# Softmax and the sum over P V by VectorE's 32x32 transposes in an attention decode kernel

## The chip, the cores and the metric

The kernel runs on one core of a Trainium2 chip. The metric is device time in microseconds for one execution of the whole program. The core's engines are called PE (TensorE matmuls; PEld is its weight load), DVE (VectorE), ACT (ScalarE), POOL (GpSimd) and SP (SyncE, which here only issues loads).

## What is computed

The reference is one decode step (one token, batch 8, width 512) of an attention layer followed by a small MLP.

```
x = A_x                                           # [8, 1, 512]
q = (layernorm(x) @ wq) as 32 heads of 128
k, v = the last 2048 positions of the caches, 8 kv heads, each shared by 4 q heads
p = softmax(q k^T / sqrt(128));  o = p v
h = x + o @ wo
y = layernorm(h)
x1 = y + (token shifts, all zero for one token)
h2 = gelu(layernorm(x1) @ w3) @ w4
out = h + x1 + h2
```

For each batch entry there are 32 rows of 2048 scores. The caches are bf16 and are read once: 2048 positions of 8 heads of 128 for K and V, 8 MB a batch, 64 MB in all, beside 4 MB each for wq and wo and 3.5 MB for w3 and w4.

## The kernel before

**Queues.** Every engine has a list of operations (`Engine.op`) that is written out in the order in which Python calls it; each engine runs its own list strictly in that order, and semaphore waits join the lists. All loads go out on SP's queue (`load_k`, `load_v`, `load_wo`, `load_wq`, `load_w3`, `load_w4`, L675 to L710) in the order of one string of letters, K and V alternating, then wo, w3 and w4. A K load is 2 MB: four kv heads. It goes into one of three slots and waits for the transposes (L323) of the load that had the slot. A V load has three slots too and waits for the P V product (L452) of three loads before. The last V goes into a K slot.

**Items.** A batch has two K loads and eight items, each a quarter of a load: `pe_T` turns 2048 rows of K with sixteen 128x128 transposes on PE (L323), `evict` copies them to SBUF, one half on ACT (L331) and one on DVE (L333), and `pe_QK` multiplies them with q (L343). The scores of a batch stand in one PSUM bank `S_ps[b % 2]` as 128 partitions x 512: 32 heads on 32 partitions, in four blocks of 32 partitions, and within a block in four groups `s`, so one head's scores lie in four of the partitions of a block.

**Softmax before.** `softmax_1` takes the maximum of each partition on DVE (L362). A head needs the maximum over its four partitions: `softmax_2` turns the column into a row with an fp32 matmul on PE (L366), joins the four on DVE (L368) and negates (L372); `softmax_3` turns the row back with another fp32 matmul (L376), copies it (L379), and ACT takes the exponential and its row sums (L380) into `P_sb`. `softmax_4` turns P with four PE transposes (L388) and a DVE copy (L392). `widen` multiplies by a matrix that repeats each row (L408, four matmuls of 512 columns) and masks the result with `own_f`, in three cases on DVE (L421) and in one on ACT (four operations at L418), giving `pT_sb`, the weights for P V. `softmax_5` sums L over the four partitions with an fp32 matmul (L425) and takes 1/L (L427).

**P V and O before.** `pe_PV` runs sixteen matmuls per half batch (L452) into `o_rows` or a free scores bank. The result holds four blocks of 128 columns, and each partition needs only one of them. ACT copies the bank as bf16 (L458), DVE subtracts for the low part (L459), and `pe_O` selects and adds blocks with eight matmuls (L469). DVE scales by 1/L and masks (L481) and adds four columns into `oW` (L487).

**Order.** The loop at L543 goes over items p and calls the parts of batch b at fixed distances from its last item: `A_WORK` and `B_WORK` (L538 to L541). The work of batch 6 is put back by four items (`LAG`, L542). `warm` (L429) and `warm_end` (L437) are matmuls whose result nothing uses; they stand in the last two batches and after them. `sm_pe` and `sm_dv` put the users of PSUM bank `sm` in one chain.

**After the attention.** With the last `oW` come wo (L498 to L531), the two layernorms, w3 (`pe_w3`, L608), Gelu on ACT (L634), w4 (L661), copies (L671, L673) and the store (L713). The residual rows enter the w4 sum through L651. POOL clears `qrow` for the MLP (L628) after the last O matmul.

Of the kernel before, what the change touches and what calls it, by code (L numbers as in the profile page):

```python
# [6 lines left out]
dt = mybir.dt  # L7
ACT = mybir.ActivationFunctionType
ALU = mybir.AluOpType
AX = mybir.AxisListType  # L10

B = 8
# [24 lines left out]
NPB = 3  # L37
ON_ACT = (1,)
# [36 lines left out]
def bass_sequential_preLN__sliding_block_cached__mixer_s_mlp__decode_kernel(  # L75
# [23 lines left out]
    with es:  # L99
# [8 lines left out]
        turn_b = sb([128, 128], dt.bfloat16, "turn_b")  # L108
        rows_f = sb([128, 64], dt.float32, "rows_f")
        heads_f = sb([128, H], dt.float32, "heads_f")  # L110
# [9 lines left out]
        sel_l = sb([128, 128], dt.float32, "sel_l")  # L120
        sel_o = sb([128, NS, 64], dt.bfloat16, "sel_o")
# [19 lines left out]
        P_sb = sb([128, NPB, 512], dt.bfloat16, "P_sb")  # L141
        pT_sb = sb([128, 2, NN, 128], dt.bfloat16, "pT_sb")
        PT_sb = sb([128, 512], dt.bfloat16, "PT_sb")
        wide = sb([128, KQ, 128], dt.bfloat16, "wide")
        mcol = sb([128, 1], dt.float32, "mcol")
        negcol = sb([128, B], dt.float32, "negcol")
        lcol = sb([128, B], dt.float32, "lcol")
        Mrow = sb([1, H], dt.float32, "Mrow")
        negrow = sb([1, 128], dt.float32, "negrow")
        rL = sb([128, B], dt.float32, "rL")  # L150
# [31 lines left out]
        O_ps = sm[:, 256:384]  # L182
        MROW = slice(384, 512)
        NEG = slice(384, 385)
        LB = slice(385, 386)
# [9 lines left out]
        def dma(eng, dst, src, sem, *waits):  # L195
            def f(e):
# [12 lines left out]
        e_ones = PO.op(lambda e: e.memset(ones_f[:], 1.0))  # L209
        e_qz = PO.op(lambda e: e.memset(qblk[:], 0.0))  # L210
# [20 lines left out]
        e_heads = DV.op(lambda e: e.tensor_reduce(heads_f[:, :].rearrange("p (t x) -> p t x", t=KQ),  # L231
                                                  ident_f[:, :].rearrange("p (t s x) -> p t x s", t=KQ, s=NS),
                                                  AX.X, ALU.add))
        a = ident_f[:, :]
        e_wd = DV.op(lambda e, a=a: e.tensor_copy(
            wide[:, :, :].rearrange("p n (a x) -> p (n a) x", x=KQ),
            bass.AP(tensor=a.tensor, offset=a.offset, ap=[a.ap[0], a.ap[1], [0, KQ]])))

        def spread(e, dst, src):
            a = src  # L240
            src = bass.AP(tensor=a.tensor, offset=a.offset, ap=[a.ap[0], a.ap[1], a.ap[2], [0, KQ]])
            return e.tensor_copy(dst.rearrange("p (t r x) -> p t r x", t=KQ, r=R), src)
        for s in range(NS):
            e_selo = DV.op(lambda e, s=s: spread(e, sel_o[:, s, :],
                                                 rows_f[:, :].rearrange("p (t s r) -> p s t r", t=KQ, s=NS)[:, s, :, :]),
                           e_rows)
        for q in range(NQ):
            e_sell = DV.op(lambda e, q=q: spread(e, sel_l[:, 64 * q:64 * (q + 1)],
                                                 heads_f[:, :].rearrange("p (t r q) -> p q t r", t=KQ, q=NQ)[:, q, :, :]),
                           e_heads)  # L250
# [49 lines left out]
        e_max, e_mT, e_neg, e_negps, e_negc, e_exp, e_PT, e_pT, e_Lb, e_rL = ({} for _ in range(10))  # L300
        e_ohi, e_olo, e_O, e_oX, e_oW, e_PTs, e_wide = ({} for _ in range(7))
# [49 lines left out]
        sm_at = {}  # L351

        def sm_pe(fn, *waits):
            sm_at[0] = PE.op(fn, *waits, sm_at.get(1))
            return sm_at[0]

        def sm_dv(fn, *waits):
            sm_at[1] = DV.op(fn, *waits, sm_at.get(0))
            return sm_at[1]

        def softmax_1(b):
            e_max[b] = DV.op(lambda e: e.tensor_reduce(mcol[:, :], S_ps[b % 2][:, :], AX.X, ALU.max),  # L362
                             e_QK[G * b + G - 1], e_mT.get(b - 1))

        def softmax_2(b):
            e_mT[b] = sm_pe(lambda e: e.matmul(sm[0:1, MROW], mcol[:, :], ident_f[:, :], start=True, stop=True),  # L366
                            e_max[b], e_rL.get(b - 1), e_idf)
            e = sm_dv(lambda e: e.tensor_reduce(Mrow[:, :].rearrange("o (t x) -> o t x", t=KQ),  # L368
                                                sm[0:1, MROW].rearrange("o (t s x) -> o t x s", t=KQ, s=NS),
                                                AX.X, ALU.max), e_mT[b])  # L370
            m_bc = bass.AP(tensor=Mrow[:, :].tensor, offset=0, ap=[[H, 1], [NQ * R, KQ], [0, NS], [1, NQ * R]])
            e_neg[b] = DV.op(lambda e: e.tensor_scalar(negrow[:, :].rearrange("o (t s x) -> o t s x", t=KQ, s=NS), m_bc,  # L372
                                                       -1.0, None, ALU.mult), e, e_negps.get(b - 1))

        def softmax_3(b):
            e_negps[b] = sm_pe(lambda e: e.matmul(sm[:, NEG], negrow[0:1, :], ones_f[0:1, 0:1],  # L376
                                                  start=True, stop=True), e_neg[b], e_ones)
            j = b % 2
            e_negc[b] = sm_dv(lambda e: e.tensor_copy(negcol[:, b:b + 1], sm[:, NEG]), e_negps[b])  # L379
            e_exp[b] = AC.op(lambda e: e.activation(P_sb[:, b % NPB, :], S_ps[j][:, :], ACT.Exp,  # L380
                                                    bias=negcol[:, b:b + 1], scale=1.0, accum_out=lcol[:, b:b + 1]),
                             e_negc[b], e_PT.get(b - NPB))
            free[j] = e_exp[b]

        def softmax_4(b):
            def f(e):
                for n in range(KQ):
                    ins = e.matmul(pT_ps[:, n * 128:(n + 1) * 128], P_sb[:, b % NPB, n * 128:(n + 1) * 128], ident_b[:, :],  # L388
                                   is_transpose=True)
                return ins  # L390
            e_PT[b] = sm_pe(f, e_exp[b], e_PTs.get(b - 1), e_idb)
            e_PTs[b] = sm_dv(lambda e: e.tensor_copy(PT_sb[:, :], pT_ps), e_PT[b], e_wide.get((b - 1, KQ - 1)))  # L392
# [4 lines left out]
        def bank_of(x, b=0):  # L397
            if b == LAST and x < KQ - 1:
                return 3 + x, kbank[x]
            if x % 2:  # L400
                for at in range(2):
                    if at in free:
                        return at, S_ps[at]
            return 2, o_rows

        def widen(b, x):
            at, bank = bank_of(x, b)
            e_wide[b, x] = PE.op(lambda e: e.matmul(bank[:, :], wide[:, x, :], PT_sb[:, :], start=True, stop=True),  # L408
                                 e_PTs[b], free[at], e_wd)
            a = own_f[:, :]  # L410
            own = bass.AP(tensor=a.tensor, offset=a.offset, ap=[a.ap[0], [0, KQ], [1, KQ], [0, H]])
            v = lambda t: t.rearrange("p n (t x) -> p n t x", t=KQ)
            to = v(pT_sb[:, b % 2, :, :].rearrange("p (n x) y -> p x n y", x=KQ)[:, x, :, :])
            got = v(bank[:, :].rearrange("p (n y) -> p n y", n=KQ))
            waits = e_wide[b, x], e_PV.get(NQ * (b - 2) + NQ - 1), e_own
            if x in ON_ACT:
                for t in range(KQ):
                    e = AC.op(lambda e, t=t: e.activation(to[:, :, t, :], got[:, :, t, :], ACT.Copy,  # L418
                                                          scale=own_f[:, t:t + 1]), *waits)
            else:  # L420
                e = DV.op(lambda e: e.tensor_tensor(to, got, own, ALU.mult), *waits)  # L421
            e_pT[b, x] = free[at] = e

        def softmax_5(b):
            e_Lb[b] = sm_pe(lambda e: e.matmul(sm[:, LB], sel_l[:, :], lcol[:, b:b + 1], start=True, stop=True),  # L425
                            e_exp[b], e_sell)
            e_rL[b] = sm_dv(lambda e: e.reciprocal(rL[:, b:b + 1], sm[:, LB]), e_Lb[b])  # L427

        def warm(b, count):  # L429
            def f(e):  # L430
                for n in range(count):
                    ins = e.matmul(kbank[KQ - 1], ident_b[:, :], PT_sb[:, :], start=True, stop=True)
                return ins
            if b >= LAST - 1:
                PE.op(f, e_hi[NITEM - 1])

        def warm_end(count):  # L437
            def f(e):
                for n in range(count):
                    ins = e.matmul(kbank[1], ident_b[:, :], PT_sb[:, :], start=True, stop=True)  # L440
                return ins
            PE.op(f, e_pT[LAST, 1])
# [19 lines left out]
        def pe_O(m):  # L462
# [11 lines left out]
            if m == NM - 1:  # L474
                warm_end(4)
# [274 lines left out]
```

## Time and profile before

| | |
|---|---|
| median of 3 runs | 193.98 us (193.85 to 193.98) |
| profiled execution | 193.81 us, span 192.4 us |
| granted TensorE clock, mean | 0.975 |
| read from HBM | 79.18 MB, 412 GB/s over the span |
| busy, us | PE 158.6, DVE 99.4, ACT 95.1, POOL 8.4 |
| K transposes L323 | 1024, 69.5 us |
| copies of turned K, L331 on ACT, L333 on DVE | 64 each, 65.5 and 44.3 us |
| scores L343, P V L452 | 256 and 256 matmuls |

The profile shows one execution. The span is the time from the first to the last instruction of the program; some 1.4 us of the profiled execution's time lie around it. Busy times can't simply be added or compared with the span, since engines run side by side: what counts is which wait ends last in each stage. In lines of the timeline the brackets give the idle time of the engine before the instruction and what ended it. In lines by stretches, the columns are the stretch, its length, the busy time (and number of instructions) of PE, PEld, DVE, ACT and POOL, the granted clock, the share of DMA and GB/s.

### The profile page before, as it was taken

The page shows a single profiled execution, that of the slowest core. Times are in us where ns is not written, and L with a number is a line of the kernel's source. Part 1 is how long each engine was busy: PE and PEld are TensorE (multiplying, and loading weights), DVE is VectorE, ACT ScalarE, POOL GpSimd, SP SyncE. Part 2 cuts the span into 40 slices and gives each one's busy share as a digit, 9 for nine tenths or more (in the row PEclk, how much of TensorE's full clock was granted, in tenths as well). Part 3 has the DMA queues.
Part 4 walks back from the last instruction along what each step waited for, and adds up shares of the span by engine and source line. Part 5 has one row for each costly group of instructions (what it writes and reads, how often), then busy time and mean ns, then how long its engine had stood idle before and what let it go on. Part 6 is the DMA issues. An engine that isn't in the chain of part 4 may idle for free.

```text
span 192.4 us, 4557 instructions
## 1 busy us (share of the span) xinstructions
PE 158.6 (82%) x2045; PEld 105.8 (55%) x2045; DVE 99.4 (52%) x206; ACT 95.1 (49%) x139; POOL 8.4 (4%) x17
## 2 busy tenths in 40 slices
PE   0002989998989899898999796999999999998984
PEld 0001667774667466655665575656765674455553
DVE  7710365655475537553755272655572747372432
ACT  3000467785358436753585355655673585232251
POOL 8300000000000000000000000000000000000130
PEclk9999999999999999999999997999999999999985
DMA  6999999999999999999999999999999999999992
GB/s 220 436 436 422 433 429 429 426 429 422 433 433 431 429 426 427 426 433 436 429 426 426 433 419 436 429 426 436 429 436 429 436 419 417 427 429 421 414 372 77
DMA packets 6323, 79.47 MB, mean 413 GB/s; under 512 B 656, under 2 KB 672, under 8 KB 1696
## 3 DMA queue, kind: packets, MB, share of 16 engines
q1 hardware_dynamic: 6288, 79.18, 96.8%
q8 instruction: 16, 0.26, 0.5%
q14 instruction: 3, 0.02, 0.0%
q10 hardware_dynamic: 16, 0.01, 0.0%
HBM read 79.18 MB, written 0.01 MB: 412 GB/s over the span
## 4 chain that ended last, share of the span: by engine, by line
DMA 67%; PE 26%; DVE 3%; SPq 1%; issue 1%
DMA knat<-in_A_k_cache_dram 32%; DMA w_sb<-in_B_w_dram 16%; PE kT_ps L323 13%; DMA vnat<-in_A_v_cache_dram 10%; DMA wbig<-in_A_wq_dram 9%; PE S_ps L343 4%; PE S_ps L452 2%; PE o_rows L452 2%; PE S_ps L271 2%; SPq L197 1%; PE sm L469 1%; PE S_ps L661 1%; DVE mcol L362 1%; DVE kT_sb L333 1%; DVE qblk L293 1%
## 5 line engine op out<-in xcount | busy, mean ns | idle before, releaser
L331 ACT ACTIVATE kT_sb<-kT_ps 128x1024 bf16<-128x1024 bf16 x64 | 65.5, 1025 | 34.9 <-PE kT_ps L323 34.7
L323 PE MATMUL kT_ps<-turn_b,knat 128*128 128x128 bf16 x1024 | 69.5, 222 | 7.7 <-DMA knat<-in_A_k_cache_dram 7.7
L323 PEld LDWEIGHTS kT_ps<-turn_b,knat 128*128 128x128 bf16 x1024 | 58.7, 99 | 23.2 <-DMA knat<-in_A_k_cache_dram 11.4
L333 DVE COPY kT_sb<-kT_ps 128x1024 bf16<-128x1024 bf16 x64 | 44.3, 692 | 33.7 <-PE kT_ps L323 33.0
L343 PE MATMUL S_ps<-kT_sb,qblk 128*32 128x512 bf16 x256 | 27.1, 393 | 0.7 <-DVE qblk L293 0.7
L452 PE MATMUL o_rows<-vnat,pT_sb 128*64 128x512 bf16 x128 | 15.4, 382 | 0.6 <-issue 0.6
L459 DVE TENSOR_TENSOR orow<-o_rows,orow 128x512 bf16<-128x512 f32 x8 | 5.5, 692 | 18.1 <-ACT orow L458 18.1
L452 PE MATMUL S_ps<-vnat,pT_sb 128*64 128x512 bf16 x112 | 13.4, 382 | 0.1
L459 DVE TENSOR_TENSOR qrow<-S_ps,qrow 128x512 bf16<-128x512 f32 x8 | 5.5, 692 | 14.7 <-ACT qrow L458 14.7
L458 ACT ACTIVATE orow<-o_rows 128x512 bf16<-128x512 f32 x8 | 4.8, 597 | 15.5 <-PE o_rows L452 15.5
L343 PEld LDWEIGHTS S_ps<-kT_sb,qblk 128*32 128x32 bf16 x256 | 7.2, 93 | 9.2 <-issue 5.1
L271 PE MATMUL S_ps<-wbig,xlnT 128*32 128x512 bf16 x32 | 3.6, 628 | 10.1 <-DMA wbig<-in_A_wq_dram 10.1
L458 ACT ACTIVATE qrow<-S_ps 128x512 bf16<-128x512 f32 x8 | 4.8, 597 | 12.6 <-PE S_ps L452 12.6
L452 PEld LDWEIGHTS o_rows<-vnat,pT_sb 128*64 128x64 bf16 x128 | 6.8, 110 | 6.9 <-issue 2.2
L421 DVE TENSOR_TENSOR pT_sb<-o_rows,own_f 128x512 bf16<-128x512 f32 x14 | 9.5, 681 | 0.5 <-PE o_rows L408 0.5
L277 ACT ACTIVATE qrow<-S_ps 128x512 bf16<-128x512 f32 x1 | 0.6, 597 | 17.2 <-PE S_ps L271 17.2
L452 PEld LDWEIGHTS S_ps<-vnat,pT_sb 128*64 128x64 bf16 x112 | 5.8, 110 | 6.0 <-issue 1.1
L418 ACT ACTIVATE pT_sb<-S_ps,own_f 128x128 bf16<-128x128 f32 x28 | 7.9, 373 | 1.2 <-PE S_ps L408 1.2
L628 POOL MEMSET qrow<- 128x704 bf16 x1 | 0.7, 684 | 171.9 <-PE sm L469 171.9
L271 PEld LDWEIGHTS S_ps<-wbig,xlnT 128*32 128x32 bf16 x32 | 1.2, 137 | 11.6 <-issue 11.6
L380 ACT ACTIVATE P_sb<-S_ps,negcol 128x512 bf16<-128x512 f32 x8 | 5.5, 687 | 4.3 <-DVE negcol L379 4.3
L255 PE MATMUL sm<-ident_b,xln_b 8*128 8x8 bf16 x4 | 0.3, 175 | 7.7 <-DVE xln_b L220 7.7
(112 smaller groups left out, 143.1 us busy)
## 6 DMA issues: line engine op xcount, KB each, us to landing
knat<-in_A_k_cache_dram SPq DMA_DIRECT2D x16, 2048.0 KB, 20.0
vnat<-in_A_v_cache_dram SPq DMA_DIRECT2D x15, 2048.0 KB, 19.2
wbig<-in_A_wq_dram SPq DMA_DIRECT2D x1, 4096.0 KB, 16.5
wbig<-in_A_wo_dram SPq DMA_DIRECT2D x2, 1024.0 KB, 22.5
knat<-in_A_v_cache_dram SPq DMA_DIRECT2D x1, 2048.0 KB, 19.5
wbig<-in_A_wo_dram SPq DMA_DIRECT2D x1, 2048.0 KB, 23.7
w_sb<-in_B_w_dram SPq DMA_DIRECT2D x1, 1792.0 KB, 29.4
w_sb<-in_B_w_dram SPq DMA_DIRECT2D x1, 1024.0 KB, 31.5
```

The lines of the kernel that those rows point to most:

```text
L197: e.dma_start(dst, src).then_inc(sem, 16)
L271: ins = e.matmul(S_ps[j][32 * u:32 * (u + 1), :], xlnT[:, kc, :], wq_v[:, kc, n:n + R * DH], start=(kc == 0), stop=(kc == KC - 1), tile_po ...
L323: ins = e.matmul(kT_ps[i % 2][:, n * 128:(n + 1) * 128], knat[:, j % NK, c * DH:(c + 1) * DH], turn_b[:, :], is_transpose=True)
L331: e_lo[i] = AC.op(lambda e: e.activation(kT_sb[:, i % NKT, 0:W // 2], kT_ps[i % 2][:, 0:W // 2], ACT.Copy), e_Tlo[i], e_QK.get(i - NKT))
L333: e_hi[i] = DV.op(lambda e: e.tensor_copy(kT_sb[:, i % NKT, W // 2:W], kT_ps[i % 2][:, W // 2:W]), e_Thi[i], e_QK.get(i - NKT))
L343: ins = e.matmul(S_ps[b % 2][32 * t:32 * (t + 1), :], qblk[:, b, KQ * q + t, at:at + H], kT_sb[:, i % NKT, :].rearrange("p (n t a) -> p t ...
L380: e_exp[b] = AC.op(lambda e: e.activation(P_sb[:, b % NPB, :], S_ps[j][:, :], ACT.Exp, bias=negcol[:, b:b + 1], scale=1.0, accum_out=lcol[ ...
L418: e = AC.op(lambda e, t=t: e.activation(to[:, :, t, :], got[:, :, t, :], ACT.Copy, scale=own_f[:, t:t + 1]), *waits)
L421: e = DV.op(lambda e: e.tensor_tensor(to, got, own, ALU.mult), *waits)
L452: ins = e.matmul(bank[64 * u:64 * (u + 1), :], pT_sb[:, b % 2, n, :].rearrange("p (x q) -> p q x", q=NQ)[:, q, :], v_tile(m)[:, n * 512:(n ...
L458: e_ohi[m] = AC.op(lambda e: e.activation(to[:, 0, :], bank[:, :], ACT.Copy), e_PV[m], e_O.get(m - 2))
L459: e_olo[m] = DV.op(lambda e: e.tensor_tensor(to[:, 1, :], bank[:, :], to[:, 0, :], ALU.subtract), e_ohi[m])
```

## The change

The softmax's steps across partitions no longer go through PE. DVE has a transpose that turns each 32x32 block of a tile in place of its partitions and columns. The maximum of each partition goes to column 0 of a 128x32 tile (`mblk`); DVE turns it, joins the four values of each head with a reduction, repeats the result (`alike`), and turns it back; the exponential takes its bias from there (`negM`). The row sums take the same way to 1/L (`invL`), and DVE multiplies P (kept in fp32 as `E_sb`) by it before rounding to bf16; the 1/L of the end falls away. P is turned by one DVE transpose of 128x512; one matmul with `back_b` (L408's place) brings the rows in order, and ACT writes the four masked copies into `pT_sb`. The four blocks of P V are scaled by a 0/1 column (`own_s`) and added on DVE, four operations for each half batch, and one fp32 matmul for both halves (`sel_o`) takes the place of sixteen; oX is then two operations of 64 partitions. In the list order, P's turn of the last batch comes after the additions of the half batch before. The five `warm` matmuls of batch 6 become fp32 transposes of 128x128, and unused matmuls read `qblk` instead of `PT_sb`. POOL's clearing of `qrow` waits for q's turn at the start instead of the last O matmul. No load is changed or moved in the list.

```diff
         def softmax_1(b):
-            e_max[b] = DV.op(lambda e: e.tensor_reduce(mcol[:, :], S_ps[b % 2][:, :], AX.X, ALU.max),
-                             e_QK[G * b + G - 1], e_mT.get(b - 1))
+            e = DV.op(lambda e: e.tensor_reduce(mblk[:, 0:1], S_ps[b % 2][:, :], AX.X, ALU.max),
+                      e_QK[G * b + G - 1], e_mz)
+            e = DV.op(lambda e: e.transpose(turned[:, :], mblk[:, :]), e)
+            e = DV.op(lambda e: e.tensor_reduce(joined[:, 0:NQ * R], heads(turned), AX.X, ALU.max, negate=True), e)
+            e = DV.op(lambda e: e.tensor_copy(per_s(turned), alike(joined)), e)
+            e_negc[b] = DV.op(lambda e: e.transpose(negM[:, :], turned[:, :]), e, e_exp.get(b - 1))
 
         def softmax_2(b):
...
+            j = b % 2
+            e_exp[b] = AC.op(lambda e: e.activation(E_sb[:, :], S_ps[j][:, :], ACT.Exp,
+                                                    bias=negM[:, 0:1], scale=1.0, accum_out=lblk[:, 0:1]),
+                             e_negc[b], e_P.get(b - 1), e_lz)
+            free[j] = e_exp[b]
 
         def softmax_3(b):
...
+            e = DV.op(lambda e: e.transpose(turned[:, :], lblk[:, :]), e_exp[b])
+            e = DV.op(lambda e: e.tensor_reduce(joined[:, 0:NQ * R], heads(turned), AX.X, ALU.add), e)
+            e = DV.op(lambda e: e.reciprocal(per_s(turned), alike(joined)), e)
+            e = DV.op(lambda e: e.transpose(invL[:, :], turned[:, :]), e)
+            e_P[b] = DV.op(lambda e: e.tensor_scalar(P_sb[:, :], E_sb[:, :], invL[:, 0:1], None, ALU.mult), e)
 
         def softmax_4(b):
...
+            e_PT[b] = DV.op(lambda e: e.transpose(PT_sb[:, :], P_sb[:, :]), e_P[b], e_wide.get(b - 1))
...
+        def turn_P(b):
+            at, bank = (3, kbank[0]) if b == LAST else bank_of(0)
+            e_wide[b] = PE.op(lambda e: e.matmul(bank[:, :], back_b[:, :], PT_sb[:, :], start=True, stop=True),
+                              e_PT[b], free[at], e_back)
+
+        def widen(b, t):
+            at, bank = (3, kbank[0]) if b == LAST else bank_of(0)
+            e_pT[b, t] = AC.op(lambda e: e.activation(pT_sb[:, b % 2, :, H * t:H * (t + 1)],
+                                                      bank[:, :].rearrange("p (n y) -> p n y", n=NN), ACT.Copy,
+                                                      scale=own_f[:, t:t + 1]),
+                               e_wide[b], e_PV.get(NQ * (b - 2) + NQ - 1), e_own)
+            if t == KQ - 1:
+                free[at] = e_pT[b, t]
...
         def warm(b, count):
             def f(e):
                 for n in range(count):
-                    ins = e.matmul(kbank[KQ - 1], ident_b[:, :], PT_sb[:, :], start=True, stop=True)
+                    if b == LAST:
+                        ins = e.matmul(kbank[KQ - 1], ident_b[:, :], still, start=True, stop=True)
+                    else:
+                        ins = e.matmul(kbank[KQ - 1][:, 0:128], still[:, 0:256].bitcast(dt.float32), ident_f[:, :],
+                                       is_transpose=True)
...
+            acc = oacc[:, q, :]
+            e = DV.op(lambda e: e.tensor_scalar(acc, bank[:, 0:DH], own_s[:, 0:1], None, ALU.mult),
+                      e_PV[m], e_O.get(b - 1), e_own_s)
+            for s in range(1, NS):
+                e = DV.op(lambda e, s=s: e.scalar_tensor_tensor(acc, bank[:, s * DH:(s + 1) * DH], own_s[:, s:s + 1], acc,
+                                                                ALU.mult, ALU.add), e)
+            e_acc[m] = free[at] = e
+
+        def pe_O(b):
+            if b == LAST:
                 warm_end(4)
...
+            e_O[b] = PE.op(lambda e: e.matmul(O_ps, sel_o[:, :], oacc[:, :, :].rearrange("p q d -> p (q d)"),
+                                              start=True, stop=True),
+                           e_acc[NQ * b], e_acc[NQ * b + 1], e_selo, e_oX.get(b - 1))
+            for q in range(NQ):
+                rows = slice(64 * q, 64 * (q + 1))
...
+                e_oX[b] = DV.op(lambda e, rows=rows, q=q, own=own: e.tensor_tensor(
...
-        B_WORK = (((3, softmax_4), (4, each(widen, 0)), (4, each(widen, 1)), (4, each(warm, 1)), (5, each(widen, 2)),
-                   (5, each(warm, 1)), (5, each(widen, 3)), (6, each(warm, 2)), (6, softmax_5), (6, each(warm, 1))),
-                  ((6, quad(pe_PV, 0)), (7, quad(pe_PV, 1)), (7, quad(pe_O, 0)), (8, quad(pe_O, 1))))
+        B_WORK = (((3, softmax_4), (4, turn_P), (4, each(widen, 0)), (4, each(widen, 1)), (4, each(warm, 1)),
+                   (5, each(widen, 2)), (5, each(warm, 1)), (5, each(widen, 3)), (6, each(warm, 2)), (6, each(warm, 1))),
+                  ((6, quad(pe_PV, 0)), (7, quad(pe_PV, 1)), (8, pe_O)))
...
-        e_gz = PO.op(lambda e: e.memset(qflat[:, 0:(2 * KC + FC) * 32], 0.0), e_O[NM - 1])
+        e_gz = PO.op(lambda e: e.memset(qflat[:, 0:(2 * KC + FC) * 32], 0.0), e_qblk)
```

## The prediction

> **What bounds the kernel now.** I read the first page from top to bottom, then the chain that ended last in order of time, then the timeline of its last 45 us, then the busy time by stretches.
>
> ```profile
> PE 158.6 (82%) x2045; PEld 105.8 (55%) x2045; DVE 99.4 (52%) x206; ACT 95.1 (49%) x139; POOL 8.4 (4%) x17
> DMA  6999999999999999999999999999999999999992
> ...
> q1 hardware_dynamic: 6288, 79.18, 96.8%
> q8 instruction: 16, 0.26, 0.5%
> ```
>
> PE looks busiest of the engines, but the DMA row is 9 from the second slice to the last but one: 79.18 MB flow through one queue without a break, and that alone fills 96.8% of the span. The loads go out in one order, and a load takes some 20 us from issue to landing while one of 2 MB moves in about 4.9 us (2.1 MB at 430 GB/s), so four are always under way. A load issued some us later is hidden by the three ahead of it.
>
> ```profile
> 127.79 19.22 DMA vnat<-in_A_v_cache_dram
> 147.00 0.04 issue
> 147.05 1.92 PE S_ps L452 x16
> ...
> 156.55 31.48 DMA w_sb<-in_B_w_dram
> 188.03 0.12 issue
> 188.15 1.04 PE S_ps L661 x32
> 189.20 0.21 PE S_ps L651 x8
> 189.41 0.94 PE S_ps L661 x17
> ```
>
> The chain says the end is a landing: the first piece of w4 lands at 188.03, and 64 small matmuls, the copies out and the store follow. But a second chain arrives at the same moment. The timeline shows the tail of the last batch:
>
> ```profile
> 162.36 0.69 DVE L362 TENSOR_REDUCE mcol<-S_ps 128x1 f32<-128x512 f32 x1
> 165.74 0.69 ACT L380 ACTIVATE P_sb<-S_ps,negcol 128x512 bf16<-128x512 f32 x1 [2.80 <-DVE negcol L379]
> 173.69 1.92 PE L452 MATMUL o_rows<-vnat,pT_sb 128*64 128x512 bf16 x16 [0.56 <-issue]
> 175.41 1.92 PE L452 MATMUL S_ps<-knat,pT_sb 128*64 128x512 bf16 x16
> 179.80 0.38 DVE L487 TENSOR_REDUCE oW<-oX 128x32 bf16<-128x128 f32 x1
> 185.49 1.89 PEld L608 LDWEIGHTS kT_ps<-uT,w_sb 128*128 128x128 bf16 x56 [0.58 <-DMA w_sb<-in_B_w_dram]
> 187.76 0.25 ACT L634 ACTIVATE qrow<-g_x 128x56 bf16<-128x56 f32 x1 [0.63 <-DVE g_x L632]
> 188.15 1.04 PE L661 MATMUL S_ps<-w_sb,qrow 128*32 128x128 bf16 x32 [0.68 <-DMA w_sb<-in_B_w_dram]
> ```
>
> The w3 matmuls (L608) start at 185.49, when w3 lands (156.07 + 29.4 = 185.47); PE's work ahead of them ended at 185.41. The last Gelu half ends at 188.01, the w4 piece lands at 188.03. So compute and DMA are level to within 0.1 us: a shorter attention tail gains nothing, a longer one costs its full excess.
>
> **The change part by part.**
>
> *Middle of the run.* Per batch PE loses the maximum's turn (0.38, after a wait of 0.46 for DVE), the negated row (0.38), four transposes (0.22), three of four widening matmuls (3 x 0.22), the sums (0.33) and two groups of eight O matmuls (2 x 0.6), and gains one fp32 matmul of 256 columns (about 0.6: L366's two passes of 128 columns take 0.38 together). That is 2.6 us of work and the wait off a batch of 19.5 us. DVE loses 5.0 us a batch (L368, L372, L379, L392, L421 x3, L427, L459 x2, L481) and gains 6.1: eight small operations at 0.19, the scaled P, the turn of P, eight additions at 0.35, two oX; it was busy for about 11.5 of the 19.5. ACT gives up four widenings of 0.29 and two of 0.6 and takes four copies of 0.6: level. Since DMA sets this stretch, the time worth is 0. Its cover is the queue: buffers are given back by the K transposes and by P V, and a release would have to come some 10 to 15 us late before the queue ran dry.
>
> *Setup.* DVE drops wide (0.42), heads_f (0.37) and six small copies (6 x 0.19) and adds four operations near 0.25; two POOL memsets (0.1 each) stand ahead of qblk's. All lie before 12 us, and wq lands at 17.92: 0. POOL's memset of qrow (0.68) moves from 179.4 to about 25.9, behind q's turn; nothing waits on POOL's queue there: 0. SP's order of loads is untouched.
>
> *The tail of the last batch*, walked with the rows above. I give no credit for an earlier last score matmul: its K lands at 151.8, but V for the P V ahead lands only at 147.0, so I keep 162.36 for the maximum.
> 1. Maximum 0.68, then transpose, reduce, copy, transpose. No row shows a DVE transpose. Between the 32-column copies at 0.18 and L481's 128-column operation at 0.35, I take 0.19, the 128x32 reduction at L618, as the sizes agree, and 0.03 between: 163.9 (164.6 at the upper end).
> 2. ACT does the four widening copies of the batch before (turned by about 161.5, then 4 x 0.60 from L458) and is free at 163.9. The exponential, 0.69 and 0.19 for its sum, ends at 164.8. Before it began only at 165.74, as its bias queued behind PE.
> 3. Four small DVE operations (0.9) and P times 1/L: 0.42 (the cast of 128x512 at L235, both in SBUF, the nearest) to 0.69 (L279, from PSUM): 166.1.
> 4. Now the new order on DVE: the four additions of the batch before stand ahead of P's turn. A 128x128 operation from PSUM with a second input is 0.35 (L481), the lower end 0.19: 4 x 0.35, 167.6. Turn of P, 128x512 bf16: 0.42 (L392) to 0.69 (L459); I take 0.69, as a block transpose can hardly be faster than a plain pass: 168.3.
> 5. One matmul (0.4), four ACT copies (2.4), then P V of the first half: 171.1 to 173.0. The second half's V was issued at 154.38 and takes 19.5: it lands at 173.9. So P V ends at 175.8; before, 177.3. Here the DVE costs have 0.9 us of cover.
> 6. Additions 1.4, the fp32 matmul 0.65, two oX on 64 rows (0.35 each), oW 0.4: 179.1 with gaps. Before, L487 ended at 180.18.
>
> [...]
>
> Sum: the tail reaches Wo 1.1 us earlier, and all of it is then lost to the wait for w3 at 185.47 and w4 at 188.03. With every unknown at its upper end (eight small operations 1.3, P 0.27, less the cover 0.9, the fp32 matmul 0.9 instead of 0.65) the tail is still 0.2 earlier. Change 0.0. The profiled execution took 193.81 (span 192.4 and 1.4 around it), 0.17 below the median of 193.98; the same sum against the median gives 194.0.
>
> **The rivals.**
>
> *A slow clock in the tail (slower).* With less PE work the waits grow, and the granted clock falls:
>
> ```profile
> 114.46:117.87 3.41, 1.89 (x25) 1.44 (x25) 1.22 (x5) 1.80 (x3) 0.00 (x0) 0.98 0.95 408
> 117.87:121.28 3.41, 3.41 (x33) 2.78 (x32) 1.02 (x2) 1.02 (x1) 0.00 (x0) 0.52 1.02 437
> ...
> 186.00:187.00 1.00, 1.00 (x35) 1.00 (x33) 0.22 (x1) 0.96 (x2) 1.00 (x1) 0.51 0.81 326
> ```
>
> After a stretch with 1.89 us of PE work in 3.41 (its longest wait 1.52), the next 3.41 us ran at half the clock, and sixteen transposes took 1.89 instead of 1.07. Stretches with 2.08 did not fall. In the new tail PE waits up to 0.9 us for the last V, and 2.1 if the scores come earlier than I allow, with the five replaced filler matmuls shorter too. If the last P V falls into a slow stretch, it takes some 1.6 us longer (half the rate): 0.5 past the old tail, 194.5; with step costs at their upper ends 195.5. It decides once the tail loses more than 1.1 us. Against it: a late tail has no wait, so it stays fast. The w3 matmuls themselves don't mind the clock: the second Gelu half's 28, all at half, took 0.9 us by the times at which L632 got them (186.62 and 187.51), the first 28 1.1.
> [...]
>
> *DVE beyond its rows (slower).* If the transposes cost far more than any row, say 0.6 us for each of four small ones and 1.5 for P's, steps 1 to 4 grow by 2.4; 1.6 of it passes the cover, 0.5 of that past the old tail: 194.5. Nothing in the profile speaks for it, but nothing shows the operation either.
>
> *Loads late in the middle (slower).* Slow stretches are likely in the middle too. Each costs up to 1.7 us, about what PE gives up per batch. They would have to add up to over 10 us; each us beyond is one us. Say 196.
>
> *Fewer instructions to fetch (faster).* The queue of instructions moved 16 packets, 0.26 MB, which spread over PE's 2045 matmuls and 2045 weight loads is 64 B for each, so I take them to be PE's code. Each takes about 0.93 us on one DMA engine, and the sixteen parts of the last load land in groups: seven by 187.2, two near 188.4, seven from 189.5 to 189.9. So fetched code makes some engines late, and these set the end. PE drops some 430 of 4090 instructions, one or two packets. But all seven late engines would have to lose one; then w4 lands up to 0.9 earlier and the time is 193.1.
>
> **How the numbers follow.** No change to within 0.2% (0.39 us, about what a measurement can tell here) 0.62, its own range 193.6 to 194.4. Slow clock 0.18, DVE beyond its rows 0.07, late loads 0.03: slower 0.28. Fewer fetches, or a stream that is faster for a reason I don't see: 0.10. The range 193.4 to 195.5 leaves out most of the fast case (0.08), the late loads and the worst of the others (0.10 together).
>
> **What the changed profile would show.** Right: the chain still ends in w_sb landing near 188.0, L608's idle before it is put down to DMA and grows by about 1 us, the last P V waits for its V at 173.9, PE's busy share falls to about 72%, and the clock row has more digits below 9 in the middle without effect. Wrong: the w4 matmuls wait for Gelu (ACT) and not for DMA, transposes on DVE well above 0.35 or 0.7 us, half clock around 174 to 178, a DMA slice below 9 in the middle, or a landing of w4 off 188.0 by over 0.4.

## The result: 0.8% slower, and the loads are what got slower

| | before | after |
|---|---|---|
| median | 193.88 us (193.75 to 193.98, 6 runs) | 195.47 us (195.39 to 195.55, 6 runs) |
| ratio after / before | | 1.0082, 95% interval 1.0069 to 1.0095 |
| profiled execution | 193.81 us, span 192.4 | 195.52 us, span 194.2 |

The time lies inside the predicted range, but the forecast itself, no change, did not come true: 1.6 us were added (1.3 to 1.8 by the interval). The range reached that far for a slow clock or dear DVE operations, and neither is the cause, so it is luck that the time lies in it. First the page of the changed kernel: busy time of the engines, the clock by slices, the queues and the HBM line.

```profile
PE 142.9 (74%) x1820; PEld 95.2 (49%) x1829; DVE 112.1 (58%) x274; ACT 94.7 (49%) x123; POOL 8.6 (4%) x19
...
PEclk9999999999996999999999999979999999699965
DMA  6999999999999999999999999999999999999981
...
q1 hardware_dynamic: 6288, 79.18, 96.6%
q8 instruction: 14, 0.23, 0.5%
...
HBM read 79.18 MB, written 0.01 MB: 408 GB/s over the span
```

PE lost 15.7 us of work and DVE gained 12.7, as the change says. The telling line is the quietest one: the same 6288 packets and the same 79.18 MB, the queue as full as before (96.8% then), but 408 GB/s in place of 412. Two fewer packets of instructions were fetched. The chain that ended last and the timeline of the tail, again of the changed kernel:

```profile
186.75 0.85 PE kT_ps L416 x2
187.60 1.79 PE kT_ps L578 x56
189.39 0.02 issue
189.42 0.23 DVE g_x L602
189.65 0.02 issue
189.67 0.26 ACT qrow L604
189.93 0.14 issue
190.06 1.04 PE S_ps L631 x24
```

```profile
164.06 0.69 DVE L351 TENSOR_REDUCE mblk<-S_ps 128x1 f32<-128x512 f32 x1 [0.94 <-PE S_ps L332]
165.91 0.70 ACT L360 ACTIVATE E_sb<-S_ps,negM 128x512 f32<-128x512 f32 x1
174.77 1.92 PE L427 MATMUL o_rows<-vnat,pT_sb 128*64 128x512 bf16 x16
176.50 1.92 PE L427 MATMUL S_ps<-knat,pT_sb 128*64 128x512 bf16 x16
181.40 0.38 DVE L457 TENSOR_REDUCE oW<-oX 128x32 bf16<-128x128 f32 x1
```

At the end everything stands later: the last P V starts at 176.50 (175.41 before), `oW` ends 1.6 us later, the w3 matmuls start at 187.39 (185.49), the w4 matmuls at 190.06 (188.15). The chain now ends through PE and Gelu, so a first reading would be that the changed computation became the bound. The landings say otherwise. The trace notes when each load's last part lands, in us from the start of the span:

| load | before | after | later by |
|---|---|---|---|
| wq | 17.92 | 18.03 | 0.11 |
| second K | 22.78 | 22.93 | 0.15 |
| first V | 33.59 | 34.00 | 0.41 |
| last K | 151.84 | 153.19 | 1.35 |
| last V | 173.85 | 175.28 | 1.43 |
| w3 | 185.45 | 187.22 | 1.77 |
| w4, first piece | 188.03 | 189.74 | 1.71 |
| w4, last piece | 189.87 | 191.65 | 1.78 |

The delay grows from the start of the run to its end (only the 22nd and 23rd of the forty loads, not in the table, landed 0.2 earlier than before). With three or more loads under way from 28 us on until w3 lands, that is not one stall but a slower stream. The records of the single packets show it too. Mean duration by size, in ns, of the packets of the loads' own queue (q1):

```
bytes of a packet     16384    8192    3584    4096    2048   32768 (wq)
count                  4224     256     512     384     128     128
before                614.7   309.0   140.0   160.2    84.0    1216.5
after                 618.1   315.5   143.6   162.9    85.2    1214.1
```

Rows of 3.5, 4 and 16 KB take some 3 to 4 ns more, whatever their size (by bytes, 3.5 KB would have got 0.7), and those of 8 KB 6.5 by the mean but 3 by the median; those of 2 KB take 1.2 more, and only the 128 rows of wq, the first load that fills `wbig`, none. Summed over all of the queue's packets that is 1.19 us on each of the 16 DMA engines (187.53 against 186.34 us), and the rest of the 1.8 us lies between packets. Yet the change touches no load.

What it does touch is the memory plan. `sb` hands out SBUF in the order of the calls. Ahead of `wbig` the change puts in `back_b` (256 bytes in each partition) and replaces `heads_f` (128 bytes) by `rows16` (64 bytes). So every tile that a load fills starts 192 bytes further on:

```
start in the partition, bytes      before    after
wbig                                18432    18624
knat                                51200    51392
vnat                               100352   100544
w3_sb                              149504   149696
w4_sb                              163840   164032
```

Before, all five are multiples of 256 (of 1024 even); after, all five lie 192 past one.

### The profile page after: what moved, and what is told of

It is laid out like the page before. It is cut to its first block, busy times and chain, and to the rows that moved or that the text cites. A ratio compares the mean times of both kernels' runs of the same rounds, so it can differ in the third digit from the quotient of the medians.

```text
span 194.2 us, 4150 instructions
## 1 busy us (share of the span) xinstructions
PE 142.9 (74%) x1820; PEld 95.2 (49%) x1829; DVE 112.1 (58%) x274; ACT 94.7 (49%) x123; POOL 8.6 (4%) x19
## 3 DMA queue, kind: packets, MB, share of 16 engines
q1 hardware_dynamic: 6288, 79.18, 96.6%
HBM read 79.18 MB, written 0.01 MB: 408 GB/s over the span
## 4 chain that ended last, share of the span: by engine, by line
DMA 47%; PE 28%; ACT 11%; DVE 10%; issue 2%; SPq 1%; another core or an unknown queue 0%
DMA knat<-in_A_k_cache_dram 39%; DMA wbig<-in_A_wq_dram 9%; PE kT_ps L312 8%; PE o_rows L427 6%; ACT pT_sb L392 5%; ACT kT_sb L320 4%; PE S_ps L427 4%; DVE oacc L437 3%; PE S_ps L332 3%; PE S_ps L260 2%; PE sm L444 2%; DVE oacc L434 1%; PE S_ps L631 1%; PE kT_ps L578 1%; DVE oX L451 1%
## 5 line engine op out<-in xcount | busy, mean ns | idle before, releaser
L427 PE MATMUL o_rows<-vnat,pT_sb 128*64 128x512 bf16 x128 | 16.8, 408 | 4.5 <-ACT pT_sb L392 4.5
L392 ACT ACTIVATE pT_sb<-o_rows,own_f 128x512 bf16<-128x512 f32 x28 | 17.7, 692 | 2.3 <-PE S_ps L332 1.2
L427 PEld LDWEIGHTS o_rows<-vnat,pT_sb 128*64 128x64 bf16 x128 | 8.6, 117 | 11.2 <-issue 8.1
L434 DVE TENSOR_SCALAR oacc<-o_rows,own_s 128x128 f32<-128x128 f32 x8 | 2.8, 351 | 15.3 <-PE o_rows L427 15.3
L360 ACT ACTIVATE E_sb<-S_ps,negM 128x512 f32<-128x512 f32 x8 | 5.5, 690 | 8.0 <-DVE negM L356 8.0
L266 ACT ACTIVATE qrow<-S_ps 128x512 bf16<-128x512 f32 x1 | 0.6, 597 | 17.3 <-PE S_ps L260 17.3
L437 DVE SCALAR_TENSOR_TENSOR oacc<-o_rows,own_s,oacc 128x128 f32<-128x128 f32 x24 | 8.4, 351 | 0.9
L437 DVE SCALAR_TENSOR_TENSOR oacc<-S_ps,own_s,oacc 128x128 f32<-128x128 f32 x24 | 8.4, 351 | 0.9
L434 DVE TENSOR_SCALAR oacc<-S_ps,own_s 128x128 f32<-128x128 f32 x8 | 2.8, 346 | 9.3 <-PE S_ps L427 9.3
L444 PE MATMUL sm<-oacc,sel_o 128*128 128x256 f32 x16 | 5.6, 431 | 3.1 <-DVE oacc L437 3.1
```

The source lines that it names most:

```text
L360: e_exp[b] = AC.op(lambda e: e.activation(E_sb[:, :], S_ps[j][:, :], ACT.Exp, bias=negM[:, 0:1], scale=1.0, accum_out=lblk[:, 0:1]), e_neg ...
L392: e_pT[b, t] = AC.op(lambda e: e.activation(pT_sb[:, b % 2, :, H * t:H * (t + 1)], bank[:, :].rearrange("p (n y) -> p n y", n=NN), ACT.Cop ...
L427: ins = e.matmul(bank[64 * u:64 * (u + 1), :], pT_sb[:, b % 2, n, :].rearrange("p (x q) -> p q x", q=NQ)[:, q, :], v_tile(m)[:, n * 512:(n ...
L434: e = DV.op(lambda e: e.tensor_scalar(acc, bank[:, 0:DH], own_s[:, 0:1], None, ALU.mult), e_PV[m], e_O.get(b - 1), e_own_s)
L437: e = DV.op(lambda e, s=s: e.scalar_tensor_tensor(acc, bank[:, s * DH:(s + 1) * DH], own_s[:, s:s + 1], acc, ALU.mult, ALU.add), e)
L444: e_O[b] = PE.op(lambda e: e.matmul(O_ps, sel_o[:, :], oacc[:, :, :].rearrange("p q d -> p (q d)"), start=True, stop=True), e_acc[NQ * b], ...
```

## The experiments

Theory A says that the starts of the loaded tiles cost the 1.6 us. Its rivals are that the changed computation is the bound (the chain through Gelu, or buffers given back late), and that a slow clock in the tail is: the first P V of batch 6 took 3.38 us in the profiled execution of the changed kernel, in place of 1.92.

### The changed kernel with its tiles back on multiples of 256

```diff
         rows16 = sb([128, KQ * R], dt.float32, "rows16")
+        pad = sb([128, 16], dt.float32, "pad")
```

> The changed kernel with one unused tile of 64 bytes per partition after rows16, so that the tiles the loads fill start 256 bytes further than in the kernel before (there they start at multiples of 1024 bytes) instead of 192. Nothing else differs from the changed kernel. Theory A (the stream of loads is slower because the changed sizes of the small tiles moved the destinations by 192 bytes): the loads land as before, the last K load near 151.9 instead of 153.2 and the first piece of w4 near 188.0 instead of 189.7, and the time falls from 195.5 by 0.5 to 1.5 us to 194.0 to 195.0; what stays above 193.9 is the compute tail. Rival B (the loads are late because the new work on DVE and ACT gives buffers back late or gets in the way of the stream): the loads land as in the changed kernel, w4 at 189.7, and the time stays 195.4 to 195.6.

Measured: 193.88 us (193.71 to 194.76, 10 runs), against 193.95 for the kernel before on the same chip: ratio 1.0004 (0.999 to 1.0017). An unused tile of 64 bytes takes back the whole loss. It puts `wbig` at 18688, which no power of two above 256 divides, so a multiple of 256 was enough here. The chain of this kernel:

```profile
155.27 30.38 DMA w_sb<-in_B_w_dram
185.70 1.99 PE kT_ps L579 x56
187.69 0.02 issue
187.72 0.23 DVE g_x L603
187.94 0.02 issue
187.97 0.26 ACT qrow L605
188.22 0.14 issue
188.36 1.04 PE S_ps L632 x31
```

The chain goes back to a load again: PE waits for w3, which lands at 185.66, and the w4 matmuls start at 188.36 (188.15 before). The packets of 16 KB are back at 614.7 ns, those of 3.5 KB at 140.0. With the same instructions on every engine, the stream, the tail and the time return.

### The kernel before with its tiles moved

```diff
         heads_f = sb([128, H], dt.float32, "heads_f")
+        pad = sb([128, 48], dt.float32, "pad")
```

That is 192 bytes, the shift that the change makes.

> The kernel before with one unused tile of 192 bytes per partition after heads_f, so that the loads' tiles start 192 bytes further, as in the changed kernel. No instruction is changed. Theory A: the stream takes about 1.5 us longer from end to end, the first piece of w4 lands near 189.6, and the time is 195.2 to 195.6, as long as that of the changed kernel. Rival B: 193.8 to 194.0, w4 at 188.0.

Measured: 195.52 us (195.36 to 195.56, 4 runs), ratio 1.0079 (1.0064 to 1.0094), the changed kernel's 1.0082. No instruction differs from the kernel before. Its chain of waits:

```profile
157.25 29.88 DMA w_sb<-in_B_w_dram
187.18 1.99 PE kT_ps L609 x56
...
189.70 0.14 issue
189.84 1.04 PE S_ps L662 x31
```

The w3 matmuls start 1.7 us later than in the kernel before, and they wait for the load and nothing else. So Theory A needs no help from the new computation: it is shown from both sides, by e1 and by this run.

### Other distances

```diff
         heads_f = sb([128, H], dt.float32, "heads_f")
+        pad = sb([128, 32], dt.float32, "pad")
```

> The kernel before with an unused tile of 128 bytes per partition at the same place. Theory A with a unit of 256 bytes (any start that is not a multiple of 256 costs the same): 195.2 to 195.6. Theory A with a unit of 128 bytes or less: 193.8 to 194.0. Rival B: 193.8 to 194.0.

```diff
         heads_f = sb([128, H], dt.float32, "heads_f")
+        pad = sb([128, 8], dt.float32, "pad")
```

> The kernel before with an unused tile of 32 bytes per partition after heads_f, so that all tiles that the loads fill start 32 bytes past a multiple of 256. At 64 past it took 195.5, at 128 past it 195.3, at 256 past it nothing. If any start off a multiple of 256 costs the same extra piece for each row, 195.2 to 195.6. If the cost grows as the start comes to smaller units (128, 64, 32), 195.6 to 196.2.

Each against the kernel before on its own chip:

| start past a multiple of 256 | time | ratio | cost |
|---|---|---|---|
| 0 (before) | 193.95 | | 0 |
| 128 | 195.27 (195.19 to 195.37, 4 runs) | 1.0068 (1.0053 to 1.0083) | +1.32 us |
| 192 | 195.52 (195.36 to 195.56, 4 runs) | 1.0079 (1.0064 to 1.0094) | +1.57 us |
| 32 | 195.82 (195.79 to 195.98, 4 runs; before 193.87) | 1.0103 (1.0086 to 1.012) | +1.95 us |

The largest power of two that divides the start is 128, 64 and 32 in these three rows, and the median cost rises as it falls. The distance itself (32, 128, 192) gives no order. (The start called "64 past" in the last expectation is this row of 192.) One price for every unaligned start did not hold: the intervals of 128 and 32 lie just apart. That of 192 overlaps both, so the order of all three rests on the medians, and that the unit sets the price is likely, not shown. The packets set only 32 apart: those of 16 KB take 617.7 ns at 128, 617.6 at 192 and 618.9 at 32.

In share of their time the short rows are hit harder: 2.6% at 3.5 KB (143.6 ns against 140.0 at 192 past) and 0.6% at 16 KB (618.1 against 614.7). One extra piece in each row, whatever its size, would do that; that there is such a piece was not shown, and neither was why 32 was the dearest start.

### Moving w3 and w4 alone

```diff
         vnat = sb([128, NV, CQ * DH], dt.bfloat16, "vnat")
+        pad = sb([128, 48], dt.float32, "pad")
         w3_sb = sb([128, KC, F], dt.bfloat16, "w3_sb")
```

> The kernel before with the unused tile of 192 bytes behind vnat, so that only w3 and w4 (3.5 MB in 896 rows of 2 to 4 KB) start off a multiple of 256 bytes; wq, wo, K and V (75.5 MB in rows of 16 KB or more) stay where they were. If the cost is one extra piece for each row that a load writes (1.5 us over 4238 rows of 16 KB, 5.7 ns for each of the 265 rows of one DMA engine), 56 rows for each engine give 0.3 us: 194.2 to 194.3. If the cost goes by bytes, 0.07 us: 193.9 to 194.0.

Measured: 194.11 us (193.99 to 194.27, 11 runs) against 193.85, ratio 1.0014 (1.0005 to 1.0022): +0.26 us (0.10 to 0.43). By bytes, w3 and w4 would have had 0.07 of the 1.57; by rows, with the 1024 rows that the trace shows for them, about 0.3. So the time speaks for rows. But the packets agree only by half: w4's 4 KB rows went from 160.2 to 162.4 ns and its 2 KB rows from 84.0 to 84.9, while w3's 512 rows stayed at 140.3 (140.0 before), though they had gone to 143.6 when K and V were moved as well. The table of packets above is the better evidence that the price goes by rows. Why w3's rows escaped here stays open. This run also settles another doubt: a pad moves every tile behind it, those that only the engines use among them. Here all of these moved by 192 bytes, and the 16 KB rows stayed at 614.9 ns, so it is the place of K's and V's own tiles that slows their rows.

### Fillers of batch 6 as before

With the starts mended, what is the rest of the change worth? In this run the tail's unused matmuls are 512 bf16 columns again.

```diff
                 for n in range(count):
-                    if b == LAST:
-                        ins = e.matmul(kbank[KQ - 1], ident_b[:, :], still, start=True, stop=True)
-                    else:
-                        ins = e.matmul(kbank[KQ - 1][:, 0:128], still[:, 0:256].bitcast(dt.float32), ident_f[:, :],
-                                       is_transpose=True)
+                    ins = e.matmul(kbank[KQ - 1], ident_b[:, :], still, start=True, stop=True)
```

The 64-byte pad of the first experiment is in it too.

> As the changed kernel with the 64 unused bytes, and the five unused matmuls of batch 6 as 512 bf16 columns again instead of 128x128 fp32 transposes. Theory C (the slow clock, which made the first P V of batch 6 take 3.38 us, comes from too little PE work in the stretch before): that product takes 1.92 again, the granted clock is 1.0 around 165 to 169, and the tail is 1 to 1.5 us shorter than in the aligned kernel without this edit; the time is then 193.8 to 194.2, at the landing of w4. Rival (the waits for VectorE alone bring the clock down, whatever fills the gap): as the aligned kernel to within 0.2 us.

Measured: 193.84 us (193.71 to 193.98, 10 runs), ratio 0.9998 (0.9988 to 1.0007). The timeline of its tail:

```profile
163.33 0.69 DVE L352 TENSOR_REDUCE mblk<-S_ps 128x1 f32<-128x512 f32 x1 [1.05 <-PE S_ps L333]
...
165.34 1.92 PE L424 MATMUL o_rows<-vnat,pT_sb 128*64 128x512 bf16 x16 [1.09 <-ACT pT_sb L393]
...
170.03 2.42 ACT L393 ACTIVATE pT_sb<-kT_ps,own_f 128x512 bf16<-128x512 f32 x4 [4.17 <-PE kT_ps L388]
...
174.32 1.92 PE L424 MATMUL S_ps<-knat,pT_sb 128*64 128x512 bf16 x16
179.65 1.26 PE L465 MATMUL kT_ps<-wbig,oW 128*32 128x512 bf16 x20 [0.39 <-DVE oW L454]
185.60 1.98 PE L575 MATMUL kT_ps<-uT,w_sb 128*128 128x8 bf16 x56 [0.78 <-DMA w_sb<-in_B_w_dram]
```

P V of batch 6 is at full speed again, as the clock theory said, and from the last maximum to wo the tail is 1.5 us shorter than in the first experiment, as it said too. But wo starts only 0.08 earlier than there, since the maximum started 1.45 later (163.33 against 161.88): here the clock was half from 128.1 to 131.6, where the first experiment's was not. The time is the same. wo starts 0.59 us earlier than in the kernel before (180.24), and the idle time ahead of the w3 matmuls is 0.78 us and put down to the load. What the tail gains is waited away at w3.

### No fillers in the last two batches

```diff
-            if b >= LAST - 1:
+            if False:
                 PE.op(f, e_hi[NITEM - 1])
```

The changed kernel with the 64-byte pad; the matmuls left out are `warm`'s, whose results nothing uses.

> The changed kernel with its load tiles on multiples of 256 bytes and without any of the unused matmuls of batches 6 and 7 (those after the attention stay). Theory C (the tail has little slack against a slow clock stretch, and the fillers keep it away): at least half of the times are 194.3 or more, the granted clock is 0.5 somewhere between 160 and 178, and the last P V comes later than 175.0. Rival (the slow stretch costs no more than the slack before w3, as in the profile of the aligned kernel, where the first P V of batch 6 took 3.47 us and the time was still 193.9): 193.7 to 194.0 in nearly all runs.

Measured: 193.90 us (193.65 to 194.53, 12 runs), ratio 1.0006 (0.9997 to 1.0015). Three of the twelve took 194.41 to 194.53, the rest 193.65 to 194.02. Both theories missed, one expecting half or more of the runs to be long and the other nearly none. The profiled execution was one of the long ones:

```profile
165.23 3.55 PE L428 MATMUL o_rows<-vnat,pT_sb 128*64 128x512 bf16 x16 [2.27 <-ACT pT_sb L393]
...
175.72 1.92 PE L428 MATMUL S_ps<-knat,pT_sb 128*64 128x512 bf16 x16
...
189.12 1.05 PE L632 MATMUL S_ps<-w_sb,qrow 128*32 128x128 bf16 x32 [0.68 <-ACT qrow L605]
```

w4's first piece landed at 188.09, so here Gelu, not a load, is what ends last: the one trace in which the tail sets the end beside an undisturbed stream, 0.6 us past the others. Its clock was half twice, from 127.6 to 131.0 and from 165.2 to 168.6, and from the K that lands at 127.4 on its chain holds no load, so both stretches count: wo starts at 181.05. The traces of the two experiments before have one such stretch each between 100 and 180 us, and wo at 179.73 and 179.65. So by these three traces the wait for w3 absorbs one slow stretch and not two. For the long runs that have no trace this is not shown. With the fp32 fillers (first experiment) two of ten runs took 194.7, with the bf16 fillers none of ten. These are small numbers; that the bf16 fillers prevent it is likely, not shown.

### Loads of the weights ahead of the last K and V

If the end of the stream hides the new computation, moving wo, w3 and w4 ahead of the last 14 loads of K and V takes the cover away: then nothing lands after the last V.

```diff
-        for kind in "KQKK" + 9 * "VK" + "VKKVKVKVVVOVOO":
+        for kind in "KQKK" + 9 * "VK" + "OOOWVKKVKVKVVVV":
...
+            if kind == "W":
+                load_w3()
+                for n in range(3):
+                    load_w4(n)
+                continue
...
-        load_w3()
-        for n in range(3):
-            load_w4(n)
```

The first run has this in the kernel before, the second in the kernel of the bf16 fillers.

> The kernel before with the order of its loads changed: wo, w3 and w4 go out before the last fourteen K and V loads, so that the last thing to land is the last half of V and everything after its P V is compute alone. The bytes are the same. Estimate from the profile of before: the stream ends near 189.9, and from the start of the last P V (175.41) to the end of the span (192.4) it took 17.0, with under 0.2 of waits for w3 and w4: some 206.7 of span, 208 us of time. All theories expect this of it; it is the base for the next run.

> The changed kernel with its load tiles back on multiples of 256 bytes and bf16 fillers in batch 6, and the same order of loads as the run before this one. It shows the changed tail behind the last P V with no load to hide it. By the prediction's step 6 (four additions of 0.35, one fp32 matmul, two oX, in place of ACT's copy, the subtraction and eight matmuls) it is 0.35 us longer than the same order in the kernel before; by the traces of the two aligned kernels (from the end of the last P V to the first wo matmul 3.4 against 2.9) 0.5 longer. Rival (the new tail is shorter, as fewer instructions and no ACT in it suggest): 0.3 to 1 us shorter.

Measured: 213.84 us (213.83 to 213.87, 4 runs) for the computation before, 211.59 (211.05 to 212.97, 4 runs) for the changed one: ratios to the kernel before of 1.1032 (1.1016 to 1.1048) and 1.0926 (1.0898 to 1.0955). Both are longer than the 208 that I had worked out, since the last V, which landed at 190.0 and 190.1, was not what P V waited for: from a K that lands at 146.1 on, the chain of either kernel holds no load, and the engines' own work sets the time. Two lines of the first timeline and two of the second:

```profile
195.62 1.92 PE L452 MATMUL S_ps<-knat,pT_sb 128*64 128x512 bf16 x16
...
200.45 1.26 PE L498 MATMUL kT_ps<-wbig,oW 128*32 128x512 bf16 x20
```

```profile
193.35 1.92 PE L424 MATMUL S_ps<-knat,pT_sb 128*64 128x512 bf16 x16
...
198.68 1.26 PE L465 MATMUL kT_ps<-wbig,oW 128*32 128x512 bf16 x20 [0.39 <-DVE oW L454]
```

Where no load covers it, the changed computation reaches its last P V 2.27 us earlier, 2.06 of it behind the start of the last maximum (182.58 and 182.37). The clock was half from 130 to 150.5 in both. Behind the last P V, it needs 5.33 us to wo in place of 4.83: the eight additions, the fp32 matmul and two oX cost 0.5 more than the two copies and eight matmuls a half that they replaced. The rest of the 2.25 us lies after wo: the clock is half from 205.0 on in the first and from 205.1 on in the second, ahead of the w3 matmuls of the one (205.85) and near the end of the other's (203.68 to 205.6). So by these two traces the new softmax, from the last maximum to the last P V, is the shorter one by some 2 us, and in the order of loads that the kernel has, none of it is seen.

## Why the prediction was wrong, and where it was right

**The failed step** is in the setup: "SP's order of loads is untouched", at a cost of 0. The order was untouched, and from that I took the stream's rate, with w3 at 185.47 and w4 at 188.03 in every sum. I read the hunks that declare tiles as bookkeeping. They moved all the loaded tiles by 192 bytes, and that is +1.57 us in the kernel before without any other edit, of the 1.6 measured. The rivals had no such case; the nearest, "loads late in the middle", was about buffers that come back late, and K and V were issued in time. The prediction had named the mark of its failure, "a landing of w4 off 188.0 by over 0.4": it was 189.74. A second mark came too, the w4 matmuls waiting for Gelu, but by 0.3 us only (190.06). That the stream sets the time held all the more: it passed its own loss on in full.

**DMA-bound, so the rest is worth nothing:** right. With the starts mended the change can't be told from none, with ratios of 1.0004 (0.999 to 1.0017) with the fp32 fillers and 0.9998 (0.9988 to 1.0007) with the bf16 ones.

**The tail, 1.1 us earlier at Wo:** right in direction, half in size: 0.5 to 0.6 (wo at 179.73 in the first experiment and 179.65 with the bf16 fillers, for 180.24). Step by step, with DVE's durations of the changed kernel:

```profile
165.49 0.21 DVE L356 STREAM_TRANSPOSE negM<-turned 128x32 f32<-128x32 f32 x1
166.73 0.21 DVE L366 STREAM_TRANSPOSE turned<-lblk 128x32 f32<-128x32 f32 x1 [1.03 <-ACT E_sb L360]
166.98 0.20 DVE L367 TENSOR_REDUCE joined<-turned 128x8 f32<-128x32 f32 x1
167.22 0.35 DVE L368 RECIPROCAL turned<-joined 128x32 f32<-128x32 f32 x1
167.85 0.49 DVE L370 TENSOR_SCALAR P_sb<-E_sb,invL 128x512 bf16<-128x512 f32 x1
169.98 1.12 DVE L437 SCALAR_TENSOR_TENSOR oacc<-o_rows,own_s,oacc 128x128 f32<-128x128 f32 x3
171.02 0.70 DVE L373 STREAM_TRANSPOSE PT_sb<-P_sb 128x512 bf16<-128x512 bf16 x1
```

- Steps 1 and 3 (0.19 for each small operation, 0.42 to 0.69 for P): the transposes took 0.21, the reductions 0.20, P 0.49; only the reciprocal, at 0.35, was underestimated. Step 4 (0.69 for the turn of P, 0.35 for an addition): 0.70, and 0.35 each by the page's groups. The rival "DVE beyond its rows" falls.
- Steps 4 and 5, the mis-sized ones: P's turn was to end at 168.3 and the last P V at 175.8, with 0.9 us of cover. The turn ended at 169.5 (bf16 fillers) and 169.6 (fp32 fillers), and the last P V at 176.2 to 176.3. In one (bf16 fillers), the maximum started at 163.33 and not at 162.36: the half clock from 128.1 to 131.6 stretched a P V to 2.97 us, and PE stayed 1.35 behind the other kernel up to the last transposes of K (159.87 against 158.52). In both, PE's list has the last score matmuls behind the matmul that waits 0.86 for VectorE's turn of the batch before, a wait that the change brought in and that I had not walked. In the other (fp32 fillers) the maximum started at 161.88, but P V of batch 6 was at the slow clock and the additions, which stand ahead of P's turn on DVE, waited for it until 167.50. Either way the widened copies end at 172.5, after them P V's first half starts at 172.6, and the second half at 174.3 follows the first and no longer the landing of its V at 174.0. That is 0.5 of the missing 0.5 to 0.6.
- Step 6 (3.3 us from P V's end to `oW`): 3.4 in the first experiment, from 176.32 to 179.68; 0.5 more than before, as I had it to 0.1. The fp32 matmul was put at 0.65 and took 0.70.

**The rival of the slow clock** was seen in the trace and is no cause of this result. Stretches of the changed kernel's tail, the columns as in the stretches of the prediction (stretch, length, busy PE, PEld, DVE, ACT, POOL, clock, DMA share, GB/s):

```profile
162.35:165.76 3.41, 1.19 (x9) 0.68 (x10) 2.28 (x7) 2.19 (x5) 0.00 (x0) 1.00 0.96 401
165.76:169.18 3.42, 3.00 (x16) 1.52 (x18) 1.47 (x5) 0.94 (x3) 0.00 (x0) 0.50 1.06 446
```

After a stretch with 1.19 us of PE work, with a wait of 1.58 at its end, the next ran at half the clock and P V of batch 6 took 3.38. But the kernel with its tiles mended has the same slow stretch (3.47) and takes 193.88: the wait for w3 absorbs it, and in the one traced run where it does not, it costs 0.6 us. I had set it on the last P V; it falls on the batch before. The wait at the end of the stretch ahead was under 1.6 us in both kernels (1.58, and 1.57 with mended tiles).

**Fewer instructions to fetch:** the packets fell from 16 to 14 as taken, and the first piece of w4 landed at 188.07 to 188.21 in the kernels with mended starts, not earlier than 188.03. That rival falls.

## What to carry to other kernels

When a kernel is bound by loads, read a diff's tile declarations as part of the load path: work out the SBUF start of every loaded tile before and after, and keep them on multiples of 256 bytes, with a pad where small tiles ahead of them change (here a shift of 192 bytes took 1.57 us of 194, and one of 256 nothing that could be told, 193.88 against 193.95). If the same bytes in the same packets take longer and the landings drift from the start of the run, look at the placement before the engines; a one-line pad in the old kernel tells in one run whether the placement does. A shorter computation behind a full queue is only worth something once the queue is shorter, so what it is really worth must be measured with the cover taken away (here 211.59 against 213.84 us without it, and a ratio of 0.9998 with it).

## What was not expected of the hardware

- The start of the loads' destinations in SBUF set part of the time: nothing that could be told 256 bytes further on (193.88 against 193.95 us), +1.32 us (0.7%) for a stream of 79 MB when the starts divide by 128 only, +1.57 (0.8%) by 64 only, +1.95 (1.0%) by 32 only. At 192 past, a row of 3.5, 4 or 16 KB took 2.7 to 3.6 ns longer (143.6, 162.9 and 618.1 ns against 140.0, 160.2 and 614.7). Whether it is the unit that orders these three, why wq's rows of 32 KB took no longer (1214.1 ns against 1216.5), and why w3's rows escaped when they were moved without K and V, is not settled.
- Reciprocal on DVE of 128x32 fp32 took 0.35 us where a copy of the same tile took 0.18; a DVE transpose of that tile took 0.21, and one of 128x512 bf16 0.70, where plain passes over 128x512 in the kernel before took 0.42 (the copy at L392) and 0.69 (the subtraction at L459).
- In the tail of the changed kernel and its variants, P V of batch 6 ran at half the clock after waits of 1.57, 1.58 and 2.27 us, and at full speed after one of 1.09; the same program, with its tiles mended, took 193.7 to 193.9 us in eight runs of ten and 194.7 to 194.8 in two.
